# Weights put together by identity matmuls, pieces overlapped by one, and ScalarE's order fixed by the program, in a linear-attention and expert-network kernel

## The chip, the cores and the metric

One core of one Trainium2 chip. The metric is the device time of one execution in microseconds (us); smaller is better. Every kernel was run several times on the same chip as the kernel before. In the profile's lines PE is TensorE (PEld its loads of the fixed operand, ACTq and SPq the queues that issue transfers), DVE is VectorE, ACT ScalarE and POOL GpSimd; L123 is a line of that run's kernel, and brackets give the idle time of the engine just before and what ended it. PSUM is the memory in which TensorE adds up its products. The kernel before takes 734.62 us (median of 3 runs, 733.73 to 735.88).

## The reference, cut to what matters

```python
# attention: 4 batches, 8 heads, 768 positions, head dimension 48
f = 1.0 / (1.0 + np.exp(-f_logit))
for t in range(S):
    state = f[:, :, t, :, None] * state + einsum('bhd,bhe->bhde', k[:, :, t], v[:, :, t])
    y[:, :, t] = einsum('bhd,bhde->bhe', q[:, :, t], state)
x = y.transpose(0, 2, 1, 3).reshape(3072, 384)
# network: w_in 384 x 2048, w_out 2048 x 384
h = x @ w_in
g = np.maximum(h, 0) + alpha * np.minimum(h, 0)
return g @ w_out
```

All is computed in fp32. The two weight matrices, however, reach the chip as float64: they are products of a float32 array and a float64 factor. The kernel has to turn each 64-bit number into fp32 itself. It reads each weight as two 32-bit words: `hi` holds the sign, 11 exponent bits and the upper 20 mantissa bits, `lo` the other 32 mantissa bits.

## The kernel before

The program runs 12 attention steps (2 batches by 128 positions each) and one network pass for each. Both are Python generators: each `yield` is a place where the program may go on with another one. A string of letters sets the order: `P` and `S` are a step of the attention at hand, `Q` a step of the next attention, `n` a step of the network of the attention before, `w` and `v` one piece of `w_in` and of `w_out`. A digit repeats. The first four iterations have their own strings; the weights are unpacked in the first two of them, 12 pieces of 128x512 for each matrix; the other iterations share `usual`.

```python
    first = (
        "P7 S w S w S w S w S w2",
        "n w n w n w n w n w n w n2 P7 S v S v S v S v2 S v n2 v3 n v3 n",
        "n P n P n P n P n P n P n P n S n S n S2 n S Q3 n",
        "n P n P n P n P S n2 S n2 S n S n S Q4 n Q3 n",
    )
    usual = "S n Q n S n Q n S Q n S Q n Q n S Q2 n5"
    with tc.manual_schedule(engines={PE, DVE}):   # cut: ScalarE's order is the scheduler's
```

One piece of the weights. VectorE cuts out exponent and sign, ScalarE rebiases the exponent, and VectorE shifts both words' mantissa bits together into one 32-bit integer, which the last instruction converts and multiplies by the power of two:

```python
            nc.vector.tensor_scalar(e, hi, 0x7FF00000, None, ALU.bitwise_and)
            nc.scalar.activation(e, e, AF.Relu, bias=bias, scale=8.0)
            nc.vector.tensor_scalar(m, hi.bitcast(U32), 11, 0x80000000, ALU.logical_shift_left, ALU.bitwise_or)
            nc.vector.scalar_tensor_tensor(m, lo.bitcast(U32), 21, m, ALU.logical_shift_right, ALU.bitwise_or)
            nc.vector.scalar_tensor_tensor(e, hi, -0x80000000, e, ALU.bitwise_and, ALU.bitwise_or)
            nc.vector.scalar_tensor_tensor(flat[:, n:n + WP], m, 2.0 ** -31, e.bitcast(F32), ALU.mult, ALU.mult)
            yield
```

Attention, cut to the order of its parts and to ScalarE's copies:

```python
        # preparation on VectorE (7 steps), then
        # raw, qu (TensorE) -> ad (VectorE), two halves; off, pk (TensorE)
        nc.scalar.copy(ksn[:, u], pk[:, u])          # u = 0, 1
        yield
        # pd (TensorE, needs ksn) -> state (VectorE)
        yield
        nc.scalar.copy(A[s_, :, :, s_], ad[s_]...)   # four copies
        nc.scalar.copy(A[s_, ...], off[s_, ...])     # four copies
        # py (TensorE, needs A and state)
        nc.scalar.copy(y[:, u]..., py[:, u])         # u = 0, 1
        # ten transfers xT <- y, five of them issued by ScalarE; then the network may start
        yield
```

The network computes `ph` (TensorE), `neg` (ScalarE) and `g` (VectorE) for eight groups of the hidden units, then `po` in four quarters, and copies `po` to `o` on ScalarE.

## Time and profile before

| | before |
|---|---|
| time, median of 3 | 734.62 us |
| span of the profiled run | 732.2 us |
| TensorE busy | 654.6 us (89%) |
| VectorE busy | 446.5 us (61%) |
| ScalarE busy | 187.2 us (26%) |
| a later step | 52.55 us, TensorE without a gap |
| end of the first `po` | 152.83 us |
| start of the fifth attention step's `raw` | 266.39 us |

### The profile page before, as it was taken

To read this page: it belongs to the slowest core of one execution; us is meant where nothing else is said; L and a number is where in the kernel's file an instruction comes from. 1 tells how busy PE (TensorE), PEld (TensorE's weight loads), DVE (VectorE), ACT (ScalarE), POOL (GpSimd) and SP (SyncE) were. 2 spreads that over 40 slices of the span, in tenths; PEclk is the share of its full clock that TensorE was granted. 3 is DMA by queue.
4 is the path that set the end of the run, shared out by engine and by line. 5 is a ranking of instruction groups with operands and counts; after the bars stand their busy time and mean duration, and the time that the engine had idled before them with its cause. 6 is when DMAs were issued, how large, how long until landed. Compare 5 with 4: busy or idle time off the path is not lost.

```text
span 732.2 us, 17405 instructions
## 1 busy us (share of the span) xinstructions
PE 654.6 (89%) x7712; PEld 488.7 (67%) x7712; DVE 446.5 (61%) x895; ACT 187.2 (26%) x327; POOL 8.9 (1%) x42
## 2 busy tenths in 40 slices
PE   1368436889998999999999999999999999999997
PEld 0357335467677668678678678588687687687774
DVE  5969698869639588548458368279088186250020
ACT  3243114222222225114015024043041041041110
POOL 4000000000000000000000000000000000000000
PEclk9989855999999999999999999999999999999999
DMA  9244215401121022112121022022021001000000
GB/s 337 90 135 145 80 32 183 148 22 30 60 94 59 5 91 89 45 27 87 41 78 55 22 81 64 10 82 74 11 70 45 22 4 44 22 3 22 22 0 22
DMA packets 31466, 46.77 MB, mean 64 GB/s; under 512 B 3744, under 2 KB 19104, under 8 KB 31392
## 3 DMA queue, kind: packets, MB, share of 16 engines
q1 hardware_dynamic: 25536, 43.26, 18.7%
q10 hardware_dynamic: 5856, 2.40, 1.4%
q8 instruction: 61, 1.00, 0.6%
q14 instruction: 13, 0.11, 0.0%
HBM read 36.22 MB, written 4.72 MB: 56 GB/s over the span
## 4 chain that ended last, share of the span: by engine, by line
PE 78%; DVE 17%; ACT 2%; issue 1%; DMA 1%; ACTq 1%; DVEq 0%
PE ph L386 31%; PE po L402 31%; PE py L349 4%; PE py L360 3%; PE raw L259 2%; PE qu L275 2%; DVE us L210 2%; PE pk L301 2%; DVE ad L280 2%; PE pd L314 2%; DVE g L394 2%; DVE ad L266 1%; PE off L293 1%; DVE qd L193 1%; DVE w_out_sb L155 1%
## 5 line engine op out<-in xcount | busy, mean ns | idle before, releaser
L386 PE MATMUL ph<-xT,w_in_sb 128*128 128x256 f32 x1152 | 267.6, 389 | 13.0 <-DVE w_in_sb L155 8.0
L402 PE MATMUL po<-w_out_sb,g 128*128 128x384 f32 x768 | 252.6, 488 | 4.7 <-DVE w_out_sb L155 4.7
L386 PEld LDWEIGHTS ph<-xT,w_in_sb 128*128 128x128 f32 x1152 | 218.6, 193 | 50.4 <-DVE w_in_sb L155 9.4
L402 PEld LDWEIGHTS po<-w_out_sb,g 128*128 128x128 f32 x768 | 144.7, 190 | 105.1 <-DVE w_out_sb L155 8.5
L394 DVE SCALAR_TENSOR_TENSOR g<-neg,om,ph 128x256 f32<-128x256 f32 x192 | 83.2, 475 | 95.3 <-ACT neg L391 95.3
L266 DVE COPY_PREDICATED ad<-mraw,raw 128x256 f32<-128x256 int32 x96 | 42.5, 443 | 124.8 <-PE raw L259 122.3
L391 ACT ACTIVATE neg<-ph 128x512 f32<-128x512 f32 x96 | 57.1, 595 | 160.3 <-PE ph L386 128.2
L259 PE MATMUL raw<-qd,k 48*32 48x128 f32 x1536 | 31.0, 297 | 30.4 <-DVE qd L193 18.9
L408 ACT COPY o<-po 128x384 f32<-128x384 f32 x24 | 11.4, 480 | 172.0 <-PE po L402 172.0
L280 DVE COPY_PREDICATED ad<-mquad,qu 128x224 f32<-128x224 int32 (+6 forms) x168 | 50.3, 300 | 7.4
L259 PEld LDWEIGHTS raw<-qd,k 48*32 48x32 f32 x1536 | 23.9, 114 | 40.1 <-issue 35.7
L210 DVE TENSOR_TENSOR us<-us,fs 128x768 f32<-128x768 f32 (+2 forms) x72 | 44.9, 624 | 2.1
L275 PE MATMUL qu<-us,k 48*32 48x116 f32 x1536 | 29.3, 288 | 13.0 <-DVE us L210 9.9
L336 ACT COPY A<-ad 32x512 f32<-32x512 f32 x48 | 29.6, 616 | 35.5 <-DVE ad L280 34.9
L275 PEld LDWEIGHTS qu<-us,k 48*32 48x32 f32 x1536 | 23.9, 114 | 15.3 <-issue 7.0
L349 PE MATMUL py<-A,v 128*64 128x128 f32 x384 | 27.0, 300 | 2.4 <-issue 1.2
L349 PEld LDWEIGHTS py<-A,v 128*64 128x64 f32 x384 | 23.9, 152 | 6.4 <-issue 5.1
L193 DVE TENSOR_TENSOR qd<-qd,f 128x768 f32<-128x768 f32 (+2 forms) x36 | 27.3, 759 | 0.8
L199 DVE TENSOR_TENSOR us<-qd,f 128x1024 f32<-128x1024 f32 x12 | 24.1, 2009 | 0.1
L360 PE MATMUL py<-q,state 48*48 48x64 f32 x704 | 22.9, 221 | 0.0
L360 PEld LDWEIGHTS py<-q,state 48*48 48x48 f32 x704 | 21.1, 123 | 2.4 <-issue 2.4
L180 ACT ACTIVATE f<-f 128x1024 f32<-128x1024 f32 x12 | 12.7, 1057 | 36.1 <-DMA f<-in_fT 36.1
(62 smaller groups left out, 365.0 us busy)
## 6 DMA issues: line engine op xcount, KB each, us to landing
f<-in_fT SPq DMA_DIRECT2D x12, 512.0 KB, 3.8
q<-in_qT SPq DMA_DIRECT2D x12, 512.0 KB, 5.0
k<-in_kT SPq DMA_DIRECT2D x12, 512.0 KB, 3.9
w_in_raw<-in_w_in SPq DMA_DIRECT2D x12, 512.0 KB, 3.8
w_out_raw<-in_w_out SPq DMA_DIRECT2D x12, 512.0 KB, 3.5
v<-in_v SPq DMA_DIRECT2D x12, 384.0 KB, 3.3
out<-o SPq DMA_DIRECT2D x24, 192.0 KB, 2.0
xT<-y SPq DMA_DIRECT2D x36, 48.0 KB, 2.0
```

The lines of the kernel that those rows point to most:

```text
L193: nc.vector.tensor_tensor(quads(qdv[d])[:, :, d:4], quads(qdv[d - 1])[:, :, d:4], f[:, :, 1:5 - d], ALU.mult)
L210: nc.vector.tensor_tensor(us[:, :, UO[m]:UO[m] + 4 * n].rearrange("p g (i r) -> p g i r", r=4), us[:, :, skip:skip + 4 * n].rearrange("p g ...
L259: nc.tensor.matmul(raw[DB * j:DB * (j + 1), par, hp * C:(hp + 1) * C], lhsT=k[r_, g:g + DB], rhs=qd[r_, 0:4 * W].rearrange("p (d x) -> p d ...
L266: nc.vector.copy_predicated(adu, mraw[:, d].rearrange("p i r -> p (i r)").bitcast(I32).unsqueeze(1).broadcast_to((128, H, DB)), rv[:, :, d])
L275: nc.tensor.matmul(qu[DB * j:DB * (j + 1), par, hp * UW:(hp + 1) * UW], lhsT=k4[r_, g * DB:(g + 1) * DB], rhs=us[r_, g], start=True, stop= ...
L280: nc.vector.copy_predicated(ad[:, u, :, :, 4 * m:DB], mquad[:, lo:lo + n].bitcast(I32).unsqueeze(1).unsqueeze(1).broadcast_to((128, 2, HP, ...
L349: nc.tensor.matmul(py[64 * par:64 * par + 64, u, hp * C:(hp + 1) * C], lhsT=vt[:, u, hd * D:hd * D + 64], rhs=A[:, u, par * HP + hp], star ...
L360: nc.tensor.matmul(py[64 * par:64 * par + D, u, o:o + CH], lhsT=states[cc][r_, u * HP + hp], rhs=qs[r_, u, hp, cc, 0:CH], start=False, sto ...
L386: nc.tensor.matmul(ph[:, j * T:(j + 1) * T], lhsT=w_in_sb[:, kt, (f + j) * 128:(f + j + 1) * 128], rhs=xT[:, kt], start=(kt == 0), stop=(k ...
L391: nc.scalar.activation(neg, phv, AF.Relu, scale=-1.0)
L394: nc.vector.scalar_tensor_tensor(g[:, j], neg[:, j], om[:, f + j:f + j + 1], phv[:, j], ALU.mult, ALU.add)
L402: nc.tensor.matmul(po[u][:, 0:DM], lhsT=gs[f // 2][:, f % 2, u * C:(u + 1) * C], rhs=w_out_sb[:, f], start=(f == 0), stop=(f == NF - 1))
```

## The change

The intent: take VectorE, the fullest engine while the weights are unpacked, out of the joining of the two words. VectorE only isolates the upper mantissa bits as an integer. ScalarE converts this and the lower word to fp32, and TensorE adds the two in PSUM by multiplying each with the identity. The matmuls and the end of a piece are issued after the start of the next piece. In addition, ScalarE's order is now the program's, and its copies are moved in the program to suit that.

```diff
-    nc.scalar.activation(om, om, AF.Identity, bias=1.0, scale=-1.0)
+    nc.gpsimd.tensor_scalar(om, om, -1.0, 1.0, ALU.mult, ALU.add)     # ahead of POOL's memory clears
...
-            nc.vector.tensor_scalar(m, hi.bitcast(U32), 11, 0x80000000, ...)
-            nc.vector.scalar_tensor_tensor(m, lo.bitcast(U32), 21, m, ...)
-            nc.vector.scalar_tensor_tensor(e, hi, -0x80000000, e, ...)
-            nc.vector.scalar_tensor_tensor(flat[:, n:n + WP], m, 2.0 ** -31, e.bitcast(F32), ALU.mult, ALU.mult)
+            nc.vector.tensor_scalar(mi, hi, 0xFFFFF, 0x100000, ALU.bitwise_and, ALU.bitwise_or)
+            nc.scalar.copy(m, mi)
+            frac = lo.bitcast(F32)
+            nc.scalar.activation(frac, lo.bitcast(U32), AF.Copy, scale=2.0 ** -32)
+            def finish(...):
+                pm = bank(f"{name}_pm{n}")
+                nc.tensor.matmul(pm, lhsT=ident, rhs=m, start=True, stop=False)
+                nc.tensor.matmul(pm, lhsT=ident, rhs=frac, start=False, stop=True)
+                nc.vector.scalar_tensor_tensor(e, hi, -0x80000000, e, ...)
+                nc.vector.scalar_tensor_tensor(flat[:, n:n + WP], pm, 2.0 ** -20, e.bitcast(F32), ALU.mult, ALU.mult)
+            if rest is not None: rest()      # the finish of the piece before
+            rest = finish
             yield
...
# the copies A<-ad and A<-off go ahead of pk and ksn (cut); a yield is added before the y copies
...
-        "P7 S w S w S w S w S w2",
-        "n w n w n w n w n w n w n2 P7 S v S v S v S v2 S v n2 v3 n v3 n",
-        "n P n P n P n P n P n P n P n S n S n S2 n S Q3 n",
-        "n P n P n P n P S n2 S n2 S n S n S Q4 n Q3 n",
+        "P7 w S w S w S w S w S w2 S",
+        "n w n w n w n w n w n w n P n P3 v P3 S v S v S v S v S v n v n S v3 n v3 n",
+        "n P n P n P n P n P n P n P n S n S n S2 n S Q3 n S",
+        "n P n P n P n P S n2 S n2 S n S n S Q4 n S Q3 n",
-    usual = "S n Q n S n Q n S Q n S Q n Q n S Q2 n5"
+    usual = "S n Q n S n Q n S Q n S Q n Q n S Q2 n S n4"
...
-    with tc.manual_schedule(engines={PE, DVE}):
+    with tc.manual_schedule(engines={PE, DVE, Activation}):
```

More of the change, by code (lines that the diff above doesn't have):

```diff
@@ L140, in load_weights @@
         per = flat.shape[1] // ks
+        rest = None
         for n in [k * per + j for j in range(0, per, WP) for k in range(ks)]:
@@ L149, in load_weights, with finish @@
             nc.scalar.activation(e, e, AF.Relu, bias=bias, scale=8.0)
-            m = work.tile([128, WP], U32, tag="m", name=f"{name}_m{n}")
-            nc.vector.tensor_scalar(m, hi.bitcast(U32), 11, 0x80000000, ALU.logical_shift_left, ALU.bitwise_or)
-            nc.vector.scalar_tensor_tensor(m, lo.bitcast(U32), 21, m, ALU.logical_shift_right, ALU.bitwise_or)
-            nc.vector.scalar_tensor_tensor(e, hi, -0x80000000, e, ALU.bitwise_and, ALU.bitwise_or)
-            nc.vector.scalar_tensor_tensor(flat[:, n:n + WP], m, 2.0 ** -31, e.bitcast(F32), ALU.mult, ALU.mult)
+            mi = work.tile([128, WP], I32, tag="m", name=f"{name}_m{n}")
+            m = mi.bitcast(F32)
+            nc.vector.tensor_scalar(mi, hi, 0xFFFFF, 0x100000, ALU.bitwise_and, ALU.bitwise_or)
+            nc.scalar.copy(m, mi)
+            frac = lo.bitcast(F32)
+            nc.scalar.activation(frac, lo.bitcast(U32), AF.Copy, scale=2.0 ** -32)
+            def finish(n=n, hi=hi, e=e, m=m, frac=frac):
+                pm = bank(f"{name}_pm{n}")
+                nc.tensor.matmul(pm, lhsT=ident, rhs=m, start=True, stop=False)
+                nc.tensor.matmul(pm, lhsT=ident, rhs=frac, start=False, stop=True)
+                nc.vector.scalar_tensor_tensor(e, hi, -0x80000000, e, ALU.bitwise_and, ALU.bitwise_or)
+                nc.vector.scalar_tensor_tensor(flat[:, n:n + WP], pm, 2.0 ** -20, e.bitcast(F32), ALU.mult, ALU.mult)
+            if rest is not None:
+                rest()
+            rest = finish
             yield
+        rest()
+        yield
     def rows(par):
@@ L284, in attention @@
             yield
+        for j in range(NJ):
+            s_ = slice(DB * j, DB * (j + 1))
+            nc.scalar.copy(A[s_, :, :, s_], ad[s_].rearrange("p u r h t -> p u (r h) t"))
         off = pair(f"off_{i}")
@@ L294, in attention @@
                                          lhsT=kh[r_, g], rhs=q3[r_, g, 2], start=True, stop=True)
+        for cc in range(NC2):
+            s_ = slice(CH * cc, CH * cc + DB)
+            for par in range(2):
+                nc.scalar.copy(A[s_, :, par * HP:(par + 1) * HP, CH * cc + DB:CH * (cc + 1)],
+                               off[s_, par, 0:U * HP * DB].rearrange("p (u h t) -> p u h t", u=U, h=HP))
         pk = pair(f"pk_{i}")
@@ L331, in attention @@
         yield
-        for j in range(NJ):
-            s_ = slice(DB * j, DB * (j + 1))
-            nc.scalar.copy(A[s_, :, :, s_], ad[s_].rearrange("p u r h t -> p u (r h) t"))
-        for cc in range(NC2):
-            s_ = slice(CH * cc, CH * cc + DB)
-            for par in range(2):
-                nc.scalar.copy(A[s_, :, par * HP:(par + 1) * HP, CH * cc + DB:CH * (cc + 1)],
-                               off[s_, par, 0:U * HP * DB].rearrange("p (u h t) -> p u h t", u=U, h=HP))
         py = pair(f"py_{i}")
@@ L362, in attention @@
                                          start=False, stop=True, skip_group_check=True)
+        yield
         y = work.tile([128, U, HP, C], F32, tag="y", name=f"y_{i}", bufs=1)
@@ L432, in begin @@
         return attention(*steps[n], x), network(*steps[n], x)
-    with tc.manual_schedule(engines={mybir.EngineType.PE, mybir.EngineType.DVE}):
+    with tc.manual_schedule(engines={mybir.EngineType.PE, mybir.EngineType.DVE, mybir.EngineType.Activation}):
         att, net = begin(0)
```

## The prediction

> **What bounds the kernel now.** I read the busy table and the 40 slices first, then the chain that ended last in order of time, then the busy time by stage, then the timeline of four places. In order:
>
> ```profile
> PE 654.6 (89%) x7712; PEld 488.7 (67%) x7712; DVE 446.5 (61%) x895; ACT 187.2 (26%) x327; POOL 8.9 (1%) x42
> ...
> PE   1368436889998999999999999999999999999997
> ...
> DVE  5969698869639588548458368279088186250020
> ```
>
> TensorE has nines from about 180 us to the end; before that VectorE is the fuller row. The busy time by stage (start to end, length, PE, PEld, DVE, ACT, ...) gives the borders:
>
> ```profile
> 0.00:51.10 51.10, 17.79 (x456) 15.05 (x456) 37.34 (x72) 17.72 (x26) 7.63 (x32) 0.99 0.56 195
> 51.10:88.04 36.94, 27.16 (x96) 20.89 (x96) 26.62 (x53) 10.32 (x16) 0.00 (x0) 0.83 0.39 120
> 88.04:126.10 38.06, 17.41 (x457) 14.75 (x457) 35.52 (x69) 10.24 (x17) 0.12 (x1) 0.55 0.28 85
> 126.10:152.80 26.70, 22.02 (x64) 11.61 (x65) 21.58 (x41) 7.28 (x11) 0.00 (x0) 1.00 0.41 127
> ...
> 312.60:687.04 374.44, 374.44 (x4557) 280.33 (x4557) 206.70 (x428) 92.28 (x170) 0.74 (x6) 1.00 0.14 42
> ```
>
> From 260 us each step takes 52.55 us (successive steps of the chain start at 371.59 and 424.16) without a gap on TensorE. Twelve such steps are 630.6 us, so about 102 us of the 732.2 us span are TensorE idle or slow, nearly all before 153 us. There the weights are unpacked on VectorE, between two attention steps and the first network pass:
>
> ```profile
> 141.21 0.69 DVE L155 SCALAR_TENSOR_TENSOR w_out_sb<-w_out_m,w_out_e 128x512 f32<-128x512 uint32 x1
> 141.82 0.42 DVE L148 TENSOR_SCALAR w_out_e<-w_out_raw 128x512 int32<-128x512 int32 x1
> 141.96 2.23 PEld L402 LDWEIGHTS po<-w_out_sb,g 128*128 128x128 f32 x8 [1.78 <-DVE w_out_sb L155]
> ...
> 142.16 0.42 DVE L152 TENSOR_SCALAR w_out_m<-w_out_raw 128x512 uint32<-128x512 uint32 x1
> 142.28 0.72 ACT L149 ACTIVATE w_out_e<-w_out_e,bias 128x512 int32<-128x512 int32 x1 [2.00 <-DVE w_out_e L148]
> 142.61 0.69 DVE L153 SCALAR_TENSOR_TENSOR w_out_m<-w_out_raw,w_out_m 128x512 uint32<-128x512 uint32 x1
> 143.22 0.68 DVE L154 SCALAR_TENSOR_TENSOR w_out_e<-w_out_raw,w_out_e 128x512 int32<-128x512 int32 x1
> ```
>
> One piece takes 2.73 us of VectorE (141.82 to the next start at 144.55); TensorE waits for it. So the change attacks the right engine in this stretch. But every microsecond of TensorE work that finds no hole moves the end.
>
> **What the Trainium skill says.** "FP8 and Floating Point Precision", section TensorE Precision Notes: true fp32 takes four passes through the array. The trace agrees: each fp32 product is two matmul records, and 24 records of 256 columns take 5.38 us, 224 ns each; 64 of 384 columns take 20.64 us, 322 ns each. The slope is 0.77 ns a column, four cycles a column over both records at the 2.4 GHz that "TensorE: Matmul & The Clock Gate" gives. The same page (Part 1) says that the clock halves after some 3.4 us of idling, that matmuls keep program order, and that ScalarE and VectorE are strict FIFO. The trace agrees on the clock: the 64 raw records take 1.96 us at 92 us against 1.09 us later. "ScalarE: Activation LUTs", What ACT_TABLE_LOAD costs: 186 ns plus 0.833 ns an element with immediates, overlapping by 93 ns; 612 ns for 512 elements, where the trace has 595 ns for neg. "VectorE: DVE Perf Modes", Why PSUM operands drop a tier: a PSUM operand keeps fp32 at one element a cycle, which these two-tensor operations have anyway; no row shows the size penalty for the new one.
>
> **The change part by part.**
>
> VectorE, per piece: one scalar_tensor_tensor goes (0.61 us start to start, 0.70 with the wait for its own predecessor). Left are two tensor_scalar (0.33 each) and two scalar_tensor_tensor (0.72 and 0.61): 2.0 us instead of 2.73. Over 24 pieces about 17 us of VectorE.
>
> ScalarE, per piece: two more operations of 512 elements, 0.52 us each back to back; with the exponent step (0.72) about 1.75 us. With 24 x 1.04 = 25 us more it is not the bound by sum, but it is in front of each matmul.
>
> TensorE, per piece: two fp32 products of 128x512 with the identity: four records of 421 ns (224 + 256 x 0.77), so 1.7 us warm, 3.4 us cold. Over 24 pieces **41 us more**, against 102 us of holes. This is the largest number of the change. The holes have to be where the pieces are:
>
> 1. Start. The scaling of om leaves ScalarE, so its first table load and the wait for alpha (5.97 us) no longer precede the sigmoid at 7.50 us. VectorE's memory clears on POOL limit the gain: about -1 us.
>
> 2. First attention step. On ScalarE, now in program order, the four copies of ad (2.5 us) and of off (1.27) precede ksn, which released pd at 38.71 us. I chain, with the durations above: second half of ad done at about 35 us, piece 3 on ScalarE to 37.5, A copies to 41.3, ksn, pd at 42, py ended at 48.7. Then the copies of y stand behind pieces 6 and 7: their matmuls follow py, VectorE finishes piece 5 at 51.8, and ScalarE does piece 7 to 53.9. y starts at 54 instead of 47.23, so the first network products run fully at 59.2 instead of 52.55: **+6.7**. In exchange six pieces are ready.
>
> 3. Network pass and w_in. Per network piece (12 ph records, two halves of h) VectorE needed 0.79 + 2.73 = 3.5 us, TensorE 2.69. Now VectorE needs 2.8, TensorE 2.69 + 1.7 = **4.4 us**: TensorE is the bound. Chained from 62.0 (first n done): five times 4.4 to 84, the last addition and its finish to 87.3, two n to 92.7, against 87.1 before: shift so far +5.6.
>
> 4. Second attention step. VectorE alone: 16.1 us of preparation, two times 4.2 of ad, 0.79 of g, and 2.7 us of pieces: ad done at 120, before 115.2: shift +4.8. The matmuls hide here.
>
> 5. w_out and first po. From ad's end: piece 3 on ScalarE, copies and ksn take about 7 us, so pd starts near 127. Then TensorE has pd 1.1, py 2.9, nine additions 15.3 and po 20.6: 39.9 us, so 167 us at best; waits for piece 7 to 12, whose addition stands behind a quarter of po, add 2 to 4 us. I take 169, where before it was 152.9: **shift +16**.
>
> 6. Hand-over between third and fourth iteration. There the y copies are placed after the last quarter of po and its o copies, and on an in-order ScalarE cannot go before them:
>
> ```profile
> 202.54 1.07 ACT L365 COPY y<-py 128x512 f32<-128x512 f32 x2 [9.96 <-PE py L360]
> ...
> 207.81 0.70 PE L386 MATMUL ph<-xT,w_in_sb 128*128 128x256 f32 x2
> ```
>
> From y to ph 5.3 us are needed; before they lay beside po. Now y starts about 0.6 us after po's end: 5.9 us to the first ph and 1.5 us until all of xT is there, of which 1.5 us existed: I take **+4**, rather than the 6 that this sums to, as the clears and waits around could shorten it.
>
> 7. Steady steps. Before, ScalarE put its ad copies around neg as they came free; pd waited 0.04 us for ksn:
>
> ```profile
> 388.29 1.25 ACT L340 COPY A<-off 32x256 f32<-32x256 f32 x4
> ...
> 389.57 1.07 ACT L304 COPY ksn<-pk 128x512 f32<-128x512 f32 x2
> ...
> 390.39 1.15 PE L314 MATMUL pd<-v,ksn 64*64 64x48 f32 x64
> ```
>
> Now all stand behind the fourth neg: from the end of its products (386.05) 0.65 to neg's end, 2.5, 1.25, 0.6 for the first half of ksn: pd at 391.1, so up to 0.7 us of wait. I take 0.5 in eight steps: **+4**.
>
> Sum: 734.6 + 16 + 4 + 4 = 758.6. I shade it to **757 us**, as every chain above was taken with the later of two possible ends.
>
> **Rivals.** (a) *The gain is real*: VectorE was the fullest engine until 153 us and 17 us go from it; the retuned order and the matmuls, which keep the clock up where py took 3.68 us instead of 1.90, hide the 41 us. For it: the 0.55 clock between 88 and 126 us, and 16.1 us of VectorE per attention preparation, where TensorE is empty. Against it: points 3 and 5, where TensorE is already 74% and 82% busy. It would make 725 to 740 us. (b) *Only TensorE's sum counts*: the ScalarE order costs nothing, as ready work waits nowhere long; then just 3 and 5 remain and it ends at 742 to 752 us. (c) *ScalarE becomes the bound*: neg, A copies, three operations a piece in one fixed row; cold additions of 3.4 us; each waits for the other. Against it: ScalarE is 30% busy up to 152.8 us (45.6 us). It would make 765 to 775 us.
>
> **Range and chances.** 2% is 720 and 749.3 us. Below 720 TensorE would have to lose under 50 us in all, while the first 35 us and the second preparation alone lose some 45: 1%. Rival (b) with the better half of its range, and parts of (a), give 27% for within 2%. The rest, 72%, is slower. Range: 742 to 772 us.
>
> **What would show it.** Right: four records of about 420 ns per piece at the identity products; TensorE over 90% busy between first ph and end of first po; that end near 169 us; y's first copies near 54 us, behind the exponent step; a TensorE gap of 4 to 6 us before the fourth iteration's first ph; waits of pd for ksn in later steps. Wrong: identity products at half that duration (then the cost is 20 us and rival (a) wins); no wait at pd; the first po ending before 153 us. The steady step, 52.55 us, should hold except for point 7; if it moves more, another wait of the in-order ScalarE is there that I did not see.

## The result, and the profile after

The changed kernel takes **765.87 us** (median of 4 runs, 765.84 to 768.25), beside 735.25 us for the kernel before (4 runs, 733.73 to 736.41). The ratio is 1.0426, with a 95% interval of 1.0397 to 1.0455: slower by 4.3%. The result is correct. The profiled run of the changed kernel was its slowest of the four (768.25), so its trace holds some 2.4 us more than the median.

The same rows of the page, for the kernel after (the first row gives busy time, share and number of instructions; the other two are tenths in 40 equal slices):

```profile
PE 693.5 (90%) x7808; PEld 499.5 (65%) x7808; DVE 431.0 (56%) x871; ACT 212.7 (28%) x373; POOL 9.7 (1%) x43
...
PE   1577946999997899999999999999999999999997
...
DVE  4953697356943968827908728548369187051020
```

TensorE has 38.9 us more, VectorE 15.5 us less, ScalarE 25.5 us more. The 38.9 us are a net figure: the records of the identity products cover 54.1 us (26.4 for `w_in`, 27.7 for `w_out`, a little of it under the next records), while the old products take less than before, `py` for example 45.3 instead of 49.1 us, since fewer of them run slowly (the first 32 records of `py` took 3.68 us before and 2.38 after). A slice is 18.3 us before and 19.2 us after, so the first `po` ends within the ninth slice before and just past it after. Up to the eighth slice TensorE had no nine before; now the fifth and the eighth are nines, and so is the ninth. The new work fills holes, and then goes on past them.

The two stretches of the network that unpack weights, from the busy time by stage of the kernel after (start to end, length, PE, PEld, DVE, ACT, POOL, granted clock, ...):

```profile
61.27:96.50 35.23, 34.53 (x120) 24.09 (x120) 18.09 (x38) 14.96 (x24) 0.00 (x0) 0.92 0.32 95
138.34:175.19 36.85, 35.35 (x101) 18.13 (x98) 14.31 (x27) 12.41 (x22) 0.00 (x0) 1.00 0.27 79
```

TensorE is 98% and 96% busy there, VectorE 51% and 39%. The bound has moved from VectorE to TensorE, and the time of these stretches is now close to TensorE's sum. One pair of identity products in the timeline (start, duration, engine, line, operation, ... x the records of the row):

```profile
152.28 1.02 PE L161 MATMUL w_out_pm<-w_out_m,ident 128*128 128x512 f32 x2
153.14 1.06 PE L162 MATMUL w_out_pm<-w_out_raw,ident 128*128 128x512 f32 x2
154.04 1.02 PE L161 MATMUL w_out_pm<-w_out_m,ident 128*128 128x512 f32 x2
```

From start to start one piece takes 154.04 - 152.28 = 1.76 us, two records for each product.

The first attention step, on ScalarE and TensorE, in the timeline of the kernel after:

```profile
39.55 2.49 ACT L303 COPY A<-ad 32x512 f32<-32x512 f32 x4
...
43.34 1.07 ACT L328 COPY ksn<-pk 128x512 f32<-128x512 f32 x2
43.98 1.17 PE L338 MATMUL pd<-v,ksn 64*64 64x48 f32 x64 [2.83 <-ACT ksn L328]
...
55.45 0.72 ACT L150 ACTIVATE w_in_e<-w_in_e,bias 128x512 int32<-128x512 int32 x1 [3.48 <-DVE w_in_e L149]
...
57.14 1.06 ACT L380 COPY y<-py 128x512 f32<-128x512 f32 x2
```

`pd` waits 2.83 us for `ksn`, which stands behind the `A` copies, and starts at 43.98 instead of 38.71 us. The copies of `y` stand behind the three ScalarE operations of the last piece, whose exponent step begins at 55.45. `y` starts at 57.14 instead of 47.23 us.

The hand-over between the third and fourth iterations:

```profile
229.70 0.48 ACT L423 COPY o<-po 128x384 f32<-128x384 f32 x1 [11.94 <-PE po L417]
...
230.72 1.08 ACT L380 COPY y<-py 128x512 f32<-128x512 f32 x2
...
234.69 1.22 PE L401 MATMUL ph<-xT,w_in_sb 128*128 128x256 f32 x2 [4.39 <-DMA xT<-y]
```

ScalarE has waited 11.94 us for the end of `po`, with `py` long done; TensorE then stands for 4.39 us, until `y` has gone through the transfers.

A later step:

```profile
416.00 2.49 ACT L303 COPY A<-ad 32x512 f32<-32x512 f32 x4
...
418.50 1.27 ACT L317 COPY A<-off 32x256 f32<-32x256 f32 x4
419.79 1.07 ACT L328 COPY ksn<-pk 128x512 f32<-128x512 f32 x2
...
420.43 1.17 PE L338 MATMUL pd<-v,ksn 64*64 64x48 f32 x64 [0.71 <-ACT ksn L328]
```

`pd` waits 0.71 us for `ksn` in each step, where before the gap was 0.04 us. The step grows from 52.55 to 53.36 us.

Put together, the shift of the same events between the two traces:

| event | before | after | shift | predicted shift |
|---|---|---|---|---|
| scan of the first preparation | 19.77 | 20.80 | +1.0 | -1 |
| `y` copies of the first step | 47.23 | 57.14 | +9.9 | +6.8 |
| all of `xT` there, first network in flow | 52.55 | 62.75 | +10.2 | +6.7 |
| end of the first eight `ph` | 86.5 | 96.5 | +10.0 | +5.6 (from 87.1) |
| `ad` of the second step done | 115.3 | 123.7 | +8.4 | +4.8 |
| end of the first `po` | 152.83 | 175.19 | +22.4 | +16 |
| hand-over passed, `ph` in flow | 209.28 | 236.62 | +27.3 | +20 |
| fifth attention step's `raw` | 266.39 | 294.05 | +27.7 | +20 |
| end of the span | 732.2 | 766.5 | +34.3 | +24, shaded to +22.4 |

### The profile page after: what moved, and what is told of

The parts are those of the page before. It is cut to its first block, busy times and chain, and to the rows that moved or that the text cites. A ratio compares the mean times of both kernels' runs of the same rounds, so it can differ in the third digit from the quotient of the medians.

```text
span 766.5 us, 17690 instructions
## 1 busy us (share of the span) xinstructions
PE 693.5 (90%) x7808; PEld 499.5 (65%) x7808; DVE 431.0 (56%) x871; ACT 212.7 (28%) x373; POOL 9.7 (1%) x43
## 5 line engine op out<-in xcount | busy, mean ns | idle before, releaser
L401 PEld LDWEIGHTS ph<-xT,w_in_sb 128*128 128x128 f32 x1152 | 218.2, 193 | 50.4 <-DMA xT<-y 11.2
L423 ACT COPY o<-po 128x384 f32<-128x384 f32 x24 | 11.6, 482 | 195.2 <-PE po L417 195.2
L274 PE MATMUL raw<-qd,k 48*32 48x128 f32 x1536 | 29.8, 289 | 21.0 <-DVE qd L208 18.3
L363 PEld LDWEIGHTS py<-A,v 128*64 128x64 f32 x384 | 21.1, 139 | 6.5 <-issue 6.5
L338 PE MATMUL pd<-v,ksn 64*64 64x48 f32 x768 | 14.0, 221 | 12.4 <-ACT ksn L328 12.4
L338 PEld LDWEIGHTS pd<-v,ksn 64*64 64x64 f32 x768 | 12.5, 134 | 18.2 <-ACT ksn L328 17.6
L363 PE MATMUL py<-A,v 128*64 128x128 f32 x384 | 24.0, 279 | 0.0
```

The source lines that it names most:

```text
L274: nc.tensor.matmul(raw[DB * j:DB * (j + 1), par, hp * C:(hp + 1) * C], lhsT=k[r_, g:g + DB], rhs=qd[r_, 0:4 * W].rearrange("p (d x) -> p d ...
L363: nc.tensor.matmul(py[64 * par:64 * par + 64, u, hp * C:(hp + 1) * C], lhsT=vt[:, u, hd * D:hd * D + 64], rhs=A[:, u, par * HP + hp], star ...
L401: nc.tensor.matmul(ph[:, j * T:(j + 1) * T], lhsT=w_in_sb[:, kt, (f + j) * 128:(f + j + 1) * 128], rhs=xT[:, kt], start=(kt == 0), stop=(k ...
```

## The experiments

Twelve kernels were run. "e7" and the like are short for the labels below. "Before" is the median of the kernel before in the runs of the same call.

| run | built on | edit | median us (range) | ratio to before (95%) |
|---|---|---|---|---|
| e1 | after | `ksn` ahead of the `A` copies of `ad` | 763.05 (760.72 to 765.44) | 1.0375 (1.0342 to 1.0408) |
| e2 | after | hand-over: `y` ahead of the end of `po` | 761.25 (758.27 to 762.12) | 1.0343 (1.0317 to 1.0369) |
| e3 | after | `om` behind the memory clears | 766.69 (765.57 to 767.28) | 1.0422 (1.0401 to 1.0443) |
| e4 | after | joining on VectorE again | 749.18 (748.69 to 749.62) | 1.0186 (1.0170 to 1.0202) |
| e5 | after | no products, lower word dropped | 741.18 (739.30 to 742.01) | 1.0074 (1.0053 to 1.0095) |
| e6 | before | the products alone | 747.33 (745.76 to 752.11) | 1.0154 (1.0130 to 1.0178) |
| e7 | after | e1, e2 and e3 together | 753.79 (751.06 to 755.02) | 1.0249 (1.0223 to 1.0276) |
| e8 | after | lower word added as bf16 | 763.77 (763.24 to 764.74) | 1.0386 (1.0369 to 1.0403) |
| e9 | after | first `y` ahead of two pieces | 766.06 (764.34 to 767.78) | 1.0416 (1.0389 to 1.0442) |
| e10 | after | e7 with 21 mantissa bits only | 722.77 (719.96 to 725.02) | 0.9830 (0.9800 to 0.9861) |
| e11 | before | 21 mantissa bits only | 730.33 (729.30 to 732.11) | 0.9938 (0.9915 to 0.9960) |
| e12 | after | e7 with the joining on VectorE | 732.55 (731.14 to 733.49) | 0.9959 (0.9936 to 0.9982) |

All results were correct within the reference's tolerance. e7, e10, e11 and e12 ran on another chip than the other eight; the kernel before took 735.3 to 735.7 us on both, so I compare medians across them. My theory was that the loss has two parts: the products, which cannot be hidden where TensorE becomes full, and three places of ScalarE's fixed order. The rival was that only one of them counts: TensorE's sum, or ScalarE.

### The two parts apart: e4 and e6

e4 keeps everything of the change but the products: the overlap, the order and the strings stay.

```diff
-            nc.vector.tensor_scalar(mi, hi, 0xFFFFF, 0x100000, ...)
-            nc.scalar.copy(m, mi)
-            nc.scalar.activation(frac, lo.bitcast(U32), AF.Copy, scale=2.0 ** -32)
+            nc.vector.tensor_scalar(m, hi.bitcast(U32), 11, 0x80000000, ...)
             def finish(...):
-                (two identity matmuls into pm)
+                nc.vector.scalar_tensor_tensor(m, lo.bitcast(U32), 21, m, ...)
```

> The changed kernel with the unpacking of the kernel before on VectorE (the shift and two scalar_tensor_tensor more; no identity products, no casts on ScalarE), the overlap of pieces, the new schedule and the fixed ScalarE order kept. My theory, sum of products and order: the products' part goes and what stays is the order's: 735 + 1 (start) + 5.5 (hand-over) + 6.5 (steady steps) + about 5 (ksn behind the copies of A in two steps) = 753 us, 748 to 757. Rival A, the order is the whole loss: 763 us or more. Rival B, the products are the whole loss: 735 to 740 us.

e6 is the other half: the kernel before with the new unpacking including its overlap, ScalarE left to the scheduler, and one more `w` or `v` in two strings, since a piece now has a finish of its own.

```diff
-        "P7 S w S w S w S w S w2",
-        "n w n w n w n w n w n w n2 P7 S v S v S v S v2 S v n2 v3 n v3 n",
+        "P7 S w S w S w S w S w3",
+        "n w n w n w n w n w n w n2 P7 S v S v S v S v2 S v2 n2 v3 n v3 n",
```

> The other half: the kernel before with only the unpacking of the changed one (identity products, casts on ScalarE, overlap by one, one more call for each matrix), ScalarE's order left to the scheduler, nothing else of the change. My theory: the products lie on the path in the network pass among w_in and in the first po: 735 + 5 + 13 = 753 us, 748 to 760; steady steps of 52.55 us and no long gap at the hand-over. Rival A (the order is the whole loss): 730 to 738 us. Rival C (without a fixed order ScalarE places casts badly and it is worse than the changed kernel): over 766 us.

Measured: e4 takes 749.18 us, 13.5 us over its before (735.73); e6 takes 747.33, 11.6 us over and 0.7 us below the range that I gave. Both rivals fall: each part alone costs something, and neither the whole. In the traces the two parts add up: e4 ends 15.5 us later than the kernel before and e6 18.1, together 33.6, where the changed kernel has 34.3. That they add up so well is partly luck: e6's trace is its slowest run (752.11, 4.8 us over its median), and that of the changed kernel is 2.4 us over its own. In the medians they add up to 25 of 30.6 us only, so some 5 us remain that I cannot divide.

The traces also say where each part costs. With the order alone (e4), the first `po` ends 3.0 us late (155.87), the hand-over brings this to 8.7, and the later steps do the rest. With the products alone (e6), the first `ph` end 1.3 us late (87.8), the second step's `pd` is nearly in place (118.37 against 118.04), but the first `po` ends at 169.78, 17 us late. All of it is lost in the one stretch, in the busy time by stage of e6:

```profile
118.37:169.78 51.41, 45.70 (x234) 24.30 (x234) 22.21 (x42) 20.56 (x37) 0.12 (x1) 0.93 0.30 91
```

The stretch takes 51.41 us instead of 34.8, and TensorE is busy for 45.70 of it. What the products cost before this (the first `ph` is in flow at 55.68 us, 3.1 late) is won back by the second `pd`.

### The three places of the order: e1, e2, e3

e1 moves the four copies of `ad` into `A` from before `off` to behind `ksn`.

```diff
-        for j in range(NJ):
-            nc.scalar.copy(A[s_, :, :, s_], ad[s_]...)
         off = pair(f"off_{i}")
...
             nc.scalar.copy(ksn[:, u], pk[:, u])
+        for j in range(NJ):
+            nc.scalar.copy(A[s_, :, :, s_], ad[s_]...)
         yield
```

> The changed kernel with only the four ScalarE copies of ad moved from before the copies of off to after those of ksn. My theory (program order on ScalarE holds pd back): the steady step goes from 53.36 us to 52.55 us again, so 8 x 0.81 = 6.5 us, and pd comes up to 2.5 us earlier in each of the two attention steps among the weights; 755 to 758 us in all instead of 766. Rival (only the identity products cost time, the order is harmless): less than 2 us are won, 764 us or more, and the step stays longer than 52.55 us for another reason.

Measured: 763.05 us, 2.8 us better than the changed kernel, not the 8 to 11 expected. The steady step is back at 52.56 us, which is worth 6.5 us. The first step gained nothing. Its `pd` does start earlier, in the timeline of e1:

```profile
41.57 1.17 PE L338 MATMUL pd<-v,ksn 64*64 64x48 f32 x64 [0.32 <-ACT ksn L325]
41.89 2.50 ACT L328 COPY A<-ad 32x512 f32<-32x512 f32 x4
...
44.41 0.72 ACT L150 ACTIVATE w_in_e<-w_in_e,bias 128x512 int32<-128x512 int32 x1
...
57.13 1.05 ACT L380 COPY y<-py 128x512 f32<-128x512 f32 x2
```

But the copies now stand before the fourth piece's exponent step, which starts at 44.41 (44.44 in the changed kernel), and `y` starts at 57.13 as before the edit. A copy that is moved on an engine in program order delays what it is put in front of. More is lost after that: in the profiled run TensorE waits once more for a transfer to `xT` (1.03 us, at 64.66 us), the first `ph` end at 99.04 instead of 96.53 us, and the fifth step's `raw` starts at 297.13 us, 3 us later than in the changed kernel. One profile cannot tell whether the edit causes that. Two of the four runs of e1 took 761 us and two 765, and the profiled one is of the slower two (764.72), so part of the missing gain comes and goes from run to run.

e2 lets the last attention step of the third iteration go before the last quarter of `po`:

```diff
-        "n P n P n P n P n P n P n P n S n S n S2 n S Q3 n S",
+        "n P n P n P n P n P n P n P n S n S n S2 n S Q3 S n",
```

> The changed kernel with only the third iteration's last two entries exchanged, so that the copies of y stand before the last quarter of po and its o copies. My theory: the gap of TensorE before the fourth iteration's first ph (about 230.3 to 237.3 us) shrinks to the 1.5 us of the kernel before; 5.5 us are won, 760.4 us. Rival: something else (the transfers of xT, SyncE's queue) holds ph, and less than 2 us are won.

Measured: 761.25 us, as expected. The lines that answer to the hand-over above, in the timeline of e2:

```profile
224.65 1.08 ACT L380 COPY y<-py 128x512 f32<-128x512 f32 x2 [7.24 <-PE py L374]
225.76 3.80 ACTq L387 DMA_DIRECT2D xT<-y  x5
229.60 0.88 ACT L423 COPY o<-po 128x384 f32<-128x384 f32 x2 [3.87 <-DMA xT<-y]
...
229.80 1.12 PE L401 MATMUL ph<-xT,w_in_sb 128*128 128x256 f32 x4
```

`y` is copied beside `po`, and the next `ph` follows `po` without a wait (229.80). A later 0.67 us remains until the rest of `xT` is there. The `o` copies now wait for the issuing of the transfers, which costs nothing here.

e3 puts the scaling of `om` behind POOL's memory clears. In the changed kernel it stands ahead of them and waits 4.68 us for `alpha`, so that the clear of `fs` ends late and VectorE waits. In the timeline of the kernel after and of e3:

```profile
6.08 0.51 POOL L93 TENSOR_SCALAR om<-om 128x16 f32<-128x16 f32 x1 [4.68 <-DMA om<-in_alpha]
...
11.00 0.61 DVE L201 TENSOR_TENSOR fs<-f,kr 128x256 f32<-128x256 f32 x1 [3.77 <-POOL fs L121]
```

```profile
9.34 0.61 DVE L201 TENSOR_TENSOR fs<-f,kr 128x256 f32<-128x256 f32 x1 [2.28 <-POOL fs L120]
```

```diff
-    nc.gpsimd.tensor_scalar(om, om, -1.0, 1.0, ALU.mult, ALU.add)
...
     nc.gpsimd.memset(A, 0.0)
+    nc.gpsimd.tensor_scalar(om, om, -1.0, 1.0, ALU.mult, ALU.add)
```

> The changed kernel with only the scaling of om moved behind POOL's memory clears instead of ahead of them. In the changed kernel POOL waits 4.7 us for alpha, its clear of fs ends at 11.0 us and VectorE's fs operation waits 3.8 us for it. My theory now (my prediction had the sign of this wrong): that clear ends near 9 us, the first preparation ends 2 us earlier (before 24 us instead of 25.8), and 2 us of it reach the end: 764 us. Rival: another input is late by the same time, and nothing is won (766).

Measured: 766.69 us, no gain in the median (the changed kernel has 765.87). The trace shows the expected: VectorE starts 1.66 us sooner, and the 1.6 us are still there at the fifth step's `raw` (292.43 us) and at the end of the span (764.9 against 766.5). But the changed kernel's trace is of its slowest run. An effect of 1.6 us is inside the spread of these runs; it stays open whether it is worth anything.

### A fourth place that failed: e9

In the first step, `y` waits for the last two pieces' ScalarE work. e9 puts it in front.

```diff
-        "P7 w S w S w S w S w S w2 S",
+        "P7 w S w S w S w S w S2 w2",
```

> The changed kernel with only the first copies of y placed ahead of the sixth and seventh piece instead of behind them. My theory: the copies start near 52.4 us when py ends, instead of 57.1; the first network products run fully near 58 us instead of 62.75; as TensorE is the bound from there on, what the two pieces take in the gap counts for nothing and 3 to 5 us are won: 761 to 763 us. Rival: the two pieces then stand in the way of the first network pieces, and under 1 us is won.

Measured: 766.06 us, no gain; the rival named there is true. ScalarE in the timeline of e9:

```profile
52.82 1.08 ACT L380 COPY y<-py 128x512 f32<-128x512 f32 x2 [2.87 <-PE py L374]
53.93 3.32 ACTq L387 DMA_DIRECT2D xT<-y  x5
57.29 0.72 ACT L150 ACTIVATE w_in_e<-w_in_e,bias 128x512 int32<-128x512 int32 x1 [3.39 <-DMA xT<-y]
```

`y` starts 4.3 us sooner, but ScalarE is then held for 3.32 us by the issuing of its five transfers. The two pieces' steps follow from 57.29, the products of the first of them run on TensorE from 58.58 to about 62.2 (3.6 us, twice the usual time), and the first `ph`, behind them in TensorE's order, starts at 62.16 instead of 61.27 us. What stood in front of `y` now stands in front of `ph`.

### The products' price: e5, e8 and e7

e5 drops the lower word. No casts and no products remain; the integer goes to the last instruction directly.

```diff
-            nc.scalar.copy(m, mi)
-            nc.scalar.activation(frac, lo.bitcast(U32), AF.Copy, scale=2.0 ** -32)
-                (two identity matmuls into pm)
-                nc.vector.scalar_tensor_tensor(flat[:, n:n + WP], pm, 2.0 ** -20, ...)
+                nc.vector.scalar_tensor_tensor(flat[:, n:n + WP], mi, 2.0 ** -20, ...)
```

> The changed kernel without the identity products and without ScalarE's two casts: the lower word is left out, VectorE multiplies the 21 mantissa bits directly (four operations a piece, as in the changed kernel). Weights are then cut at 2 to the power of -20, wrong on purpose in the last bits. My theory: all the 41 us of TensorE go, VectorE stays at 2.0 us a piece; against the same with five VectorE operations this wins up to 0.7 us in the some 17 pieces on the path: about 741 us, 735 to 746. Rival: if ScalarE's order and the waits between engines were what bounds the weight stages, then over 750 us.

Measured: 741.18 us, as expected. The first `po` ends at 147.9 us, 27 us sooner than with the products, and the trace's remaining loss of 6.8 us lies in the later steps (0.71 us of `pd` in each), as in e4 and the changed kernel.

e8 asks whether a cheaper product would do. The lower word counts only from the 21st bit on, so bf16 is enough for it.

```diff
-            frac = lo.bitcast(F32)
+            frac = (raw as bf16, every fourth element: the low half of lo)
...
-                nc.tensor.matmul(pm, lhsT=ident, rhs=frac, start=False, stop=True)
+                nc.tensor.matmul(pm, lhsT=ident16, rhs=frac, start=False, stop=True)
```

> The changed kernel with the lower word's fraction written as bf16 and added by a bf16 identity (it needs few bits, as it lies under the 21 bits of the upper word), so that the second product should take a quarter of the first's time: TensorE 1.07 us a piece instead of 1.71, 15 us less in sum. My theory (TensorE is the bound in the network pass among w_in and in the first po, with some 15 pieces there): 9 us are won, 757 us, 754 to 760. Rival (pieces wait for ScalarE and VectorE, not for TensorE's time): under 3 us.

Measured: 763.77 us, 2 us better, not the expected 9. Two things went wrong. The bf16 product is one record rather than two, but this record takes 0.43 us, so half of the fp32 product's time, not a quarter. And ScalarE's conversion became twice as long. How the shortfall divides between the two was not tested. The timeline of e8 on TensorE, and the group of the conversion in e8 and in the kernel after (count, busy us, mean ns, idle before):

```profile
70.23 0.61 PE L164 MATMUL w_in_pm<-w_in_raw,ident 128*128 128x512 bf16 x1
...
70.66 2.12 PE L403 MATMUL ph<-xT,w_in_sb 128*128 128x256 f32 x9
...
L159 ACT ACTIVATE w_out_raw<-w_out_raw 128x512 bf16<-128x512 uint32 x12 | 16.2, 1348 | 0.0
```

```profile
L157 ACT ACTIVATE w_out_raw<-w_out_raw 128x512 f32<-128x512 uint32 x12 | 8.0, 668 | 0.0
```

Both operands step by 8 bytes, as the words are interleaved. Whether a dense bf16 operand would do better was not run.

e7 is the changed kernel with e1, e2 and e3 together, so the products in the best order that I found; its edit is those three diffs.

> The changed kernel with its identity products, and three order repairs together: copies of ad behind those of ksn, y ahead of o at the hand-over, om last on POOL. My theory (order and products are separate parts): 766 - 6.5 - 6 - 1.6 = 752 us, 749 to 755, with a steady step of 52.55 us; what is left over the kernel before, some 17 us, is the products' and cannot be ordered away. Rival (the products only cost because the order is bad): 740 us or less.

Measured: 753.79 us (before 735.34), as expected: 12.1 us better than the changed kernel, and still 18.5 us over the kernel before.

### What the fixed order and the overlap are worth by themselves: e12, e11, e10

e12 is e7 with VectorE's exact joining, the edit of e4.

> The same three repairs with VectorE's own unpacking, exact as in the kernel before: 749 - 6.8 - 5.6 - 1.6 = 735 us, 731 to 739: a fixed ScalarE order costs nothing in itself, only its misplaced entries do. Rival (fixing ScalarE's order has a price of its own, for example an early wait that blocks later work): over 741 us.

Measured: 732.55 us, 0.4% below the kernel before (the interval, 0.9936 to 0.9982, excludes 1). So the fixed order of ScalarE, together with the overlap and the new strings, costs nothing once its copies stand in the right places. And e7 minus e12, 21.2 us, is what products and casts cost in the same order beyond the VectorE operation that they save.

e11 and e10 drop VectorE's second joining operation without any products: 21 bits of the mantissa, with half a unit added against the truncation (and the exponent's bias lowered by 20, since the integer is 2^20 times the mantissa). A weight is then off by up to about half of 2^-20, some 5e-7 of its size. This is not the same kernel in accuracy. e11 does it in the kernel before, e10 in e7's order and overlap.

```diff
+            nc.vector.tensor_scalar(mi, hi, 0xFFFFF, 0x100000, ALU.bitwise_and, ALU.bitwise_or)
             nc.vector.scalar_tensor_tensor(e, hi, -0x80000000, e, ...)
+            nc.vector.scalar_tensor_tensor(flat[:, n:n + WP], mi, 0.5, e.bitcast(F32), ALU.add, ALU.mult)
```

> The kernel before with only that one VectorE operation a piece left out (21-bit mantissa, rounded), ScalarE's order left to the scheduler. Without products and without order costs, what the removed operation is worth by itself: the vector-unpack and no-products runs differed by 8 us in the median and 8.7 in the span for 24 x 0.7 = 17 us of VectorE, so 735 - 9 = 726 us, 722 to 730. Rival (VectorE's time is not on the path, as waits take its place): 733 us or more.

> The three repairs, and the lower word left out altogether: four VectorE operations a piece, no products, the 21-bit mantissa rounded by half a unit (weights to about 5e-7 instead of fp32's 6e-8; wrong in the last bits on purpose). Sum of the parts measured so far: 741 - 6.8 - 5.6 - 1.6 = 727 us, 723 to 731, so faster than both kernels. If the parts do not add, over 733 us.

Measured: e11 730.33 us, 5.0 below its before and about half of what I expected; e10 722.77 us, 9.8 below e12, just under the range that I gave. e10 also shows the gross price of the trade: e7 differs from it by the products and the casts (the rest is constants), and takes 31.0 us more, of which the saved VectorE operation gives 9.8 back. No run has the casts without the products, so these two are not told apart. The same instruction was removed 24 times in both. The group of the sign operation tells the difference (count, busy us, mean ns, then idle time of VectorE just before it and what ended it). In the kernel before:

```profile
L154 DVE SCALAR_TENSOR_TENSOR w_in_e<-w_in_raw,w_in_e 128x512 int32<-128x512 int32 x12 | 8.2, 687 | 5.5 <-ACT w_in_e L149 5.3
L154 DVE SCALAR_TENSOR_TENSOR w_out_e<-w_out_raw,w_out_e 128x512 int32<-128x512 int32 x12 | 8.2, 686 | 2.9 <-ACT w_out_e L149 2.8
```

in e11:

```profile
L153 DVE SCALAR_TENSOR_TENSOR w_in_e<-w_in_raw,w_in_e 128x512 int32<-128x512 int32 x12 | 8.3, 692 | 12.5 <-ACT w_in_e L149 12.5
L153 DVE SCALAR_TENSOR_TENSOR w_out_e<-w_out_raw,w_out_e 128x512 int32<-128x512 int32 x12 | 8.3, 692 | 9.7 <-ACT w_out_e L149 9.7
```

in e10:

```profile
L156 DVE SCALAR_TENSOR_TENSOR w_out_e<-w_out_raw,w_out_e 128x512 int32<-128x512 int32 x12 | 8.2, 685 | 2.5 <-ACT w_out_e L150 2.5
L156 DVE SCALAR_TENSOR_TENSOR w_in_e<-w_in_raw,w_in_e 128x512 int32<-128x512 int32 x12 | 8.2, 684 | 0.0
```

In e11 VectorE waits 12.5 + 9.7 = 22.2 us for ScalarE's exponent step, against 8.1 us (5.3 + 2.8) in the kernel before: 14 us of some 17 removed come back as this wait, in which the removed operation had been lying. With the next piece started before the last one is finished (e10), 2.5 us of it are left. e10 differs from e11 in ScalarE's order too, but it is the overlap that removes this wait: e6 has the overlap with the scheduler's order, and there the same two groups wait 1.8 us for the exponent step, in e4 and e12 0.0. **The overlap by one is the good part of the change**, as far as this wait shows (no run has the overlap alone, so its share of the time is not measured); it pays once VectorE's operation really goes and TensorE does not take the work. e10 is the fastest kernel, at lower accuracy; e12 is the fastest exact one.

## Why the prediction was right

The direction and the mechanism held: slower, at 765.87 us, within the range of 742 to 772 and above the point of 757. The two traces differ by 34.3 us where the working had 24 (and 22.4 after shading). Point by point:

- **VectorE, ScalarE, TensorE sums.** Predicted -17, +25 and +41 us; measured -15.5, +25.5 and +38.9. That the last two numbers are so close is partly luck: I priced every product at full clock and nothing else on TensorE, but the products cover 54.1 us, because five of the 24 pieces ran slowly, and the old products take some 12 us less, because fewer of those did. So rival (a) was right that the products keep the clock up; it does not make good for them. The 612 ns of an operation on ScalarE, and the 0.52 us back to back, were estimates from the page's formula; in the trace the two new operations take 603 and 671 ns on average, and follow each other after 0.51 us. The new last operation, which reads PSUM, takes 692 ns, the same as the one it replaces.
- **Identity products.** Predicted 1.7 us a piece, measured 1.76 warm; the first ones at 27.6 us took 3.7, where I had 3.4 for a slow clock. My slope of 0.77 ns a column is only 3.7 cycles over both records, not four; with the 440 ns a record measured at 512 columns it is 0.84 ns, and four. The network's period with a piece, predicted 4.4 us, was 4.35 (`ph` bursts at 68.75, 73.10, 77.44, 81.79, 86.14 us).
- **Point 1, start: wrong sign.** I had POOL's clears limit the gain to 1 us, but did not see that `om` itself now stands in front of them and waits for `alpha`: +1.0 us instead of -1.
- **Point 2, first step: mis-sized.** The order of the steps was right, but `pd` began at 43.98 instead of 42 and `y` at 57.14 instead of 54. The 2 us at `pd` are point 1's error, which this chain takes over: it had the second half of `ad` done at about 35 us, and that was 37.5. From `pd` to `y` it had 12 us, measured are 13.2. The chain I drew let ScalarE run the pieces back to back. In the trace each piece's exponent step waits for VectorE (3.48 us at 55.45), VectorE for the products (3.19 us at 54.26), and these stand behind `py` in TensorE's order. +10.2 instead of +6.7.
- **Points 3 and 4** held in their lengths: from the first `ph` in flow to the end of the eight `ph` 33.8 us (predicted 33.5), from there to `ad` 27.2 (predicted 27.3, though the items that I listed sum to 28.0). The shifts I gave for them are off by 0.6 us, as I had read 87.1 us for the end of the eight `ph` before, where the trace has 86.5.
- **Point 5: mis-sized.** From `ad` to the end of `po` the shift grew by 14.0 us, predicted 11.2. The place was right (e6 loses its 17 us exactly here), and so were the `A` copies before `ksn`: `pd` followed `ad` after 6.5 us, predicted 7. TensorE's sum was too small. From `pd` to the end of `po` it was busy for 42.91 us instead of 39.9, mainly since the nine additions took 17.9 us and not 15.3: 1.76 to 1.87 us each, and the one at 131.95, which ran slowly, 3.5. The waits came to 2.1 us, as assumed.
- **Point 6** held in place; its size was taken too small: +4.9 in the trace (27.3 - 22.4), where I had worked out 6 and written 4. e2 gives 4.6 us back in the medians.
- **Point 7**: 0.71 us of wait was the upper end of the range I had given and I took 0.5. Eight steps of 0.81 us make 6.5 us instead of 4. e1 shows that this wait is the copies' order and nothing else.
- **The shading** from 758.6 to 757 went the wrong way. I gave as reason that every chain took the later end; in fact point 1 left out the wait for `alpha`, point 2 that of the pieces for each other, and point 5 the slow addition.
- **The signs I named.** The product records, the end of `po` past 153, the gap at the hand-over and the waits of `pd` all came. One was badly worded: "over 90% between first `ph` and end of first `po`" is not met, as the second preparation lies between, where TensorE is busy for 17.09 of 33.71 us. Over the whole it is 83% (93.30 of 112.44 us); in the two network stretches it is 98% and 96%.
- **Small readings.** TensorE's row has an eight between 220 and 238 us, after "nines to the end". For `raw` the 1.96 us are a row of the timeline and the 1.09 us a step of the chain; the timeline's row in later steps is 1.16 us. That matmuls keep program order stands in Part 2 of the page named, not in Part 1.

Rival (a), that the gain is real, is refuted by the result and by e6: with products, casts and overlap the kernel before is 11.6 us slower. Rival (b), only TensorE's sum, is refuted by e4, where the order alone costs 13.5 us. Rival (c) gave the right number, 765 to 775, and half the reason: in the first step the engines do wait for each other in a ring. But ScalarE is not the bound (12.41 of 36.85 us busy in the stretch up to the end of the first `po`); what costs is what stands in front of what on it.

The loss can be divided by the medians: 21.2 us for the products and casts, less the saved VectorE operation, in the repaired order (e7 against e12), 12.1 us for the three places of ScalarE's order (the changed kernel against e7), and 2.8 us won by overlap, strings and fixed order (e12 against before): 21.2 + 12.1 - 2.8 = 30.5. This sum closes by construction and is no check. The division depends on the order of the steps: undoing the products first (e4) gives them 16.7 us, and the three repairs one by one (e1, e2, e3) win 2.8, 4.6 and -0.8 us, 6.6 together and not 12.1. How much of the products hides in TensorE's holes is read from e7 and e10, which differ by them and the casts: TensorE is busy for 691.7 and 649.9 us, 41.8 apart, and the times are 31.0 apart, so only some 11 us hide. All of the cost arises before the end of the first `po`, which comes at 173.66 us in e7, at 150.53 in e12 and at 141.94 in e10.

## What to carry to other kernels

Moving work to an engine with idle time helps only where the idle time is in the same stretch: here TensorE was idle for 77.6 us, but the stretch from the second `pd` to the end of the first `po`, 83% busy already, took on 17 us. When an engine's order is fixed by the program, go through every long instruction or transfer issue on it and ask what stands behind it; here three placements cost 12 us, and moving one (e9) only moved the wait. Before removing an operation, look at whether it lies in another engine's latency: the same removal was worth 5 us where each piece was finished before the next (e11), and 10 where the next was started first (e10 against e12).

## What the Trainium skill lacked or had wrong

- "ScalarE: Activation LUTs" (What ACT_TABLE_LOAD costs) gives one rate for fp32 and bf16 alike. A conversion of 512 elements, in place with a step of 8 bytes, took 668 ns with an fp32 result and 1348 ns with a bf16 result (e8). The page has nothing on the step of the output; a dense bf16 output was not run.
- "TensorE: Matmul & The Clock Gate" (Back-to-back issue gap) gives 518 cycles, 216 ns, for 512 columns at the full clock. A bf16 operand with a step of 8 bytes took 0.43 us (70.23 to 70.66 us in e8). "Advanced Engine Details and Errata" (SBUF Cachelines) says that the tolerance to strides depends on the type, and "SBUF — State Buffer" puts it at 8 elements for bf16, where e8 steps by 4; the fp32 product with the same step in bytes took 0.90 us, the dense one 0.86. That the step is the cause is not shown, as no dense bf16 product was run.
- "VectorE: DVE Perf Modes" (The TRN2 errata) gives a fixed part of 58 cycles for SBUF and 120 for PSUM sources. The two-tensor operation took 692 ns with an SBUF operand (before) and 692 ns with a PSUM operand (after): no difference. The same section's own fit for fp32 `tensor_tensor`, (N+151)/0.96, which it gives as 691 ns at 512 elements, fits both.
- "DMA: Bandwidth & Descriptors" (Latency and other measured facts) gives the time to the first byte, but no time for which the issuing engine is held; the page has only 512 cycles an instruction for "previous generations", in its table on a newer chip's faster path. Five issues in a row held ScalarE for 3.32 us in e9 and 3.80 us in e2, 0.66 to 0.76 us each, and its next instruction started only then; the two at the start of the kernel after took 0.45 and 0.50 us.
- The granted clock of the profile before was 1.00 from 13 to 36 us, while 64 `raw` records took 1.96 us there and 1.16 us in later steps. "TensorE: Matmul & The Clock Gate" (Seeing it yourself) warns that the clock's events are not reliable; here durations of a known instruction were the better clock.
